# Decode attention on one core: the first K tile loaded as two halves of the partitions, by two queues

## The chip, the cores and the metric

The kernel runs on one core of one Trainium2 chip. A core has five instruction streams: TensorE (PE, matrix products, its weight loads shown as PEld), VectorE (DVE), ScalarE (ACT), GpSimd (POOL) and SyncE (SP), which here only issues loads. They run on their own and meet at semaphores. Loads are issued by SyncE and by ScalarE, each of which has a queue of its own; 16 DMA engines move the data from the chip's memory (HBM) into the core's working memory, which has 128 partitions. The metric is the device time in microseconds (us): the median over runs, and less is better. Before the change it was 318.32 us, the median of 3 runs from 318.13 to 318.70.

## The reference

One step of decoding: 16 heads, one query row for each, 8192 keys and values of 256 numbers, all in bfloat16.

```python
B, H, Sq, Sk, D = 1, 16, 1, 8192, 256

def reference(q, k, v):
    scale = q.shape[-1] ** -0.5
    scores = jnp.einsum("bhqd,bhkd->bhqk", q, k) * scale
    p = _softmax(scores, axis=-1)
    return jnp.einsum("bhqk,bhkd->bhqd", p, v)
```

Each head's K and each head's V are 8192 x 256 x 2 bytes = 4096 KB. Every byte of them is used once.

## The kernel before, in words

**Tiles.** The 8192 keys of a head are laid over the 128 partitions, 64 consecutive keys in each (`J = 64`), so a partition's part of a head's K is one run of 64 blocks of 256 numbers, 32 KB. K has two buffers (`kbuf`, the halves for even and odd heads) and V has two (`vbuf`). One load fills a buffer; its rows are the partitions.

**The order of the loads.** SyncE issues all K and V loads in the order written out in `ORDER` (L16): k0, k1, v0, k2, v1, k3, v2 and so on to v15. `CUTS` (L15) says which tiles are cut into pieces along the 64 blocks, each piece a load of its own: k0 and k15 after block 34, and v13, v14 and v15. The first piece counts on the tile's own semaphore ("k0" is that of even heads, "k1" of odd ones), the second piece of a K tile on "kb". Before the load of head h from 2 on, SyncE waits until the buffer is free: for K until DVE has finished head h - 2 ("kd", L122) and POOL too ("tp", L123), for V until TensorE has used the V that stood there ("pr", L125). SyncE's loads share one queue and are served in the order of issue. q is loaded by ScalarE (L387), 16 rows of 512 bytes, in ScalarE's queue.

**Scores.** TensorE spreads a head's q over the 128 partitions into `qrow` (L247), and ScalarE copies it into `q_now` (`q_copy`, L351 to L356, counting "qb"). Blocks 0 to 23 of K are multiplied with `q_now` by POOL, four blocks in one instruction (L186), into `prod`, and summed by ScalarE (L398). Blocks 24 to 63 are multiplied and summed by DVE with `qrow`, one block in one instruction, in four chunks of ten (L207 to L221). POOL and DVE both begin a head with `k_waits` (L141 to L144): q copied, and the head's K tile landed. DVE's chunks also wait for "kb" (L209), which for chunk 0 of head 0 is satisfied and from chunk 1 on stands for the second piece of k0, and for head 15 likewise for that of k15. The counter "kb" starts at 16 (L22).

**The rest.** DVE takes the largest score of each partition (L229), TensorE and DVE the largest of all (L332, L203), ScalarE the exponentials (L363), and TensorE multiplies them with V (`doubles`, L270) two heads behind the scores. ScalarE and TensorE collect the head's result. The last head's V is used in pieces as they land (L334 to L347), and SyncE stores the results at the end.

**At the start.** ScalarE issues the load of q, loads its table for the exponential, copies q for head 0 (`q_copy(0)`), and enters its loop, whose first act is `q_copy(1)`. In the code `q_copy` is called with a plain number only for head 0; in the loop its argument is the loop's register.

Of the kernel before, what the change touches and what calls it, by code (L numbers as in the profile page):

```python
# [11 lines left out]
NPL = 24  # L12
GRP = 4
CH = 10
CUTS = {"k0": (0, 34), "k15": (0, 34), "v13": (0, 48), "v14": (0, 40), "v15": (0, 28, 48, 60)}  # L15
ORDER = "k0 k1 v0 k2 v1 k3 v2 k4 v3 k5 v4 k6 k7 v5 k8 v6 k9 v7 k10 v8 k11 v9 k12 v10 k13 v11 k14 v12 k15 v13 v14 v15"  # L16
LAST_PAIRED = 28
STRIP = 64
# [7 lines left out]
def bass_standalone__mha_softmax__decode_kernel(nc: bass.Bass, q: bass.AP, k: bass.AP, v: bass.AP, out: bass.AP):  # L26
    B, H, Sq, D = q.shape
    Sk = k.shape[2]
    P = 128
# [25 lines left out]
    with contextlib.ExitStack() as ctx:  # L55
# [9 lines left out]
        def sem(name):  # L65
            if name not in sems:
                sems[name] = ctx.enter_context(nc.semaphore(name))
            return sems[name]
# [37 lines left out]

        for name in ("pool", "cb", "cf", "ldq", "qp", "qb", "tp", "sp", "kd", "m", "mT", "g", "bc", "nb", "ex"):
            sem(name)
        for name in ("rc", "pr", "cm", "pv", "fin", "o"):
            sem(name)  # L110
        for _, _, _, _, name in stream:
            sem(name)
# [1 line left out]
        def src(t, h):  # L114
            return t[0, h].rearrange("(p j) d -> p (j d)", p=P)

        @(lambda f: f(nc.sync))
        def _(sp):
            for kind, h, a, b, name in stream:
                if h >= 2 and a == 0:  # L120
                    if kind == "k":
                        sp.wait_ge(sem("kd"), (h - 1) * NC)  # L122
                        sp.wait_ge(sem("tp"), (h - 1) * NG)  # L123
                    else:
                        sp.wait_ge(sem("pr"), h + 2)  # L125
                buf = kbuf[:, h % 2 * J * D :] if kind == "k" else vbuf[h % 2]
                sp.dma_start(buf[:, a * D : b * D], src(k if kind == "k" else v, h)[:, a * D : b * D]).then_inc(  # L127
                    sem(name), 16
                )
            sp.wait_ge(sem(stream[-1][-1]), 16)  # L130
            sp.wait_ge(sem("fin"), LAST + 3)
            sp.dma_start(
                out.rearrange("b h s (two d) -> two (b h s) d", two=2)[:, 0:LAST, :],
                o_all[0:WIDE:BLK, :].rearrange("two (h d) -> two h d", d=HW),
            ).then_inc(sem("o"), 16)
            sp.wait_ge(sem("fin"), H + 4)
            sp.dma_start(out[0, LAST, :, :], o_last[:, :]).then_inc(sem("o"), 16)
            sp.wait_ge(sem("o"), 32)
            sp.nop()
# [55 lines left out]
        @(lambda f: f(nc.vector))  # L195
        def _(dve):
            def recips(h, n, after=0):
                dve.wait_ge(sem("pr"), h - n + (3 + after))
                dve.reciprocal(recip[:, ds(back(h, n), 1)], tot[0:WIDE, :]).then_inc(sem("rc"), 1)  # L199

            def xmax(h, n):
                dve.wait_ge(sem("mT"), h - n + 2)
                dve.tensor_reduce(g[:, :], mx[0:1, 0:P], AX.X, ALU.max).then_inc(sem("g"), 1)  # L203

            with dve.Fori(0, H) as h:
                par = dve.snap(h % 2)
                with dve.Fori(0, NC) as c:  # L207
                    k_waits(dve, h)
                    dve.wait_ge(sem("kb"), (h * 8 + c + 119) // 120 * 16 + 16)  # L209
                    for b in range(CH):  # L210
                        col = kbuf[:, ds(par * (J * D) + c * (CH * D) + (NPL + b) * D, D)]
                        ins = dve.scalar_tensor_tensor(  # L212
                            out=col,
                            in0=col,
                            scalar=SCALE,
                            in1=qrow[:, ds(par * 512, D)],
                            op0=ALU.mult,
                            op1=ALU.mult,
                            accum_out=S[:, ds(h * J + c * CH + (NPL + b), 1)],
                        )  # L220
                    ins.then_inc(sem("kd"), 1)  # L221
                    with dve.If(c == 0):
                        with dve.If(h > 1):
                            recips(h, 2)
                        with dve.If(h > 0):
                            xmax(h, 1)
                dve.wait_ge(sem("kd"), h * NC + NC)
                dve.wait_ge(sem("sp"), h * NG + (NG + 2))
                dve.tensor_reduce(m[:, :], S[:, ds(h * J, J)], AX.X, ALU.max).then_inc(sem("m"), 1)  # L229
            recips(LAST, 1)  # L230
            xmax(LAST, 0)
            recips(LAST, 0, 1)
            dve.wait_ge(sem("pv"), H + 4)
            dve.wait_ge(sem("rc"), H + 3)
            row, a = halves[1]
            dve.tensor_scalar(
                out=o_last[:, a : a + HW],
                in0=ob[row : row + 1, 0:HW],
                scalar1=recip[0:1, LAST:H],
                scalar2=None,  # L240
                op0=ALU.mult,
            ).then_inc(sem("fin"), 1)
# [106 lines left out]
        @(lambda f: f(nc.scalar))  # L349
        def _(act):  # L350
            def q_copy(h):  # L351
                act.wait_ge(sem("qp"), h + 1)
                par = 0 if isinstance(h, int) else act.snap(h % 2)
                act.activation(out=q_now[:, ds(par * D, D)], in_=qrow[:, ds(par * 512, D)], func=ACT.Copy).then_inc(  # L354
                    sem("qb"), 1
                )  # L356

            def expo(h, n):
                act.wait_ge(sem("bc"), h - n + 2)
                act.activation(out=negb[:, :], in_=sm, func=ACT.Copy, scale=-1.0).then_inc(sem("nb"), 1)  # L360
                act.wait_ge(sem("nb"), h - n + 2)
                i = back(h, n)
                act.activation(  # L363
                    out=E[:, ds(i % 2 * EW, J)].rearrange("p (two x) -> p x two", two=2),
                    in_=S[:, ds(i * J, J)].rearrange("p (x two) -> p x two", two=2),
                    func=ACT.Exp,
                    bias=negb[:, :],
                    scale=1.0,
                    accum_out=lsum[:, :],
                ).then_inc(sem("ex"), 1)  # L370

            def collect(h, n):
                act.wait_ge(sem("pr"), h - n + 4)
                act.activation(out=comb[:, :], in_=acc[0:ROWS, :], func=ACT.Copy).then_inc(sem("cm"), 1)  # L374

            def final(h, n):
                act.wait_ge(sem("pv"), h - n + 4)
                act.wait_ge(sem("rc"), h - n + 4)
                i = back(h, n)
                act.activation(  # L380
                    out=o_all[:, ds(i * HW, HW)],
                    in_=ob[0:WIDE, 0:HW],
                    func=ACT.Copy,
                    scale=recip[:, ds(i, 1)],
                ).then_inc(sem("fin"), 1)

            act.dma_start(q_sb[:, :], q[0, :, 0, :]).then_inc(sem("ldq"), 16)  # L387
            act.preload_act_table(ACT.Exp)
            q_copy(0)
            with act.Fori(0, H + 2) as h:  # L390
                with act.If(h < H):
                    q_copy(h + 1)
                with act.Fori(0, NG) as i:
                    with act.If(h < H):
                        act.wait_ge(sem("tp"), h * NG + i + 1)
                        for b in range(GRP):
                            part = prod[:, ds(i % 2 * (GRP * D) + b * D, D)]
                            ins = act.activation(  # L398
                                out=part,
                                in_=part,  # L400
                                func=ACT.Copy,
                                scale=SCALE,
                                accum_out=S[:, ds(back(h, 0) * J + i * GRP + b, 1)],
                            )
                        ins.then_inc(sem("sp"), 1)
                    with act.If(i == 1):
                        with act.If(h > 0):
                            with act.If(h < H + 1):
                                expo(h, 1)
                        with act.If(h > 2):  # L410
                            final(h, 3)
                with act.If(h > 1):
                    collect(h, 2)
            act.wait_ge(sem("pv"), H + 4)
            act.wait_ge(sem("rc"), H + 3)
            act.activation(out=o_last[:, 0:HW], in_=ob[0:1, 0:HW], func=ACT.Copy, scale=recip[0:1, LAST:H]).then_inc(
                sem("fin"), 1
            )
            act.nop()
# [28 lines left out]
```

## Time and profile before

| | |
|---|---|
| median of 3 runs | 318.32 us (318.13 to 318.70) |
| the profiled execution | 318.05 us |
| its span, first to last instruction | 316.6 us |
| busy: DVE, POOL, ACT, PE | 232.5, 204.3, 191.2, 147.2 us |
| data moved | 134.25 MB, mean 424 GB/s over the span |
| share of the DMA engines' time, SyncE's queue | 98.9% |
| loads of 4096 KB, issue to landing (median) | K 21.1 us, V 27.1 us |

The span is cut into 40 equal slices of 7.9 us for the busy digits; a digit is the busy share of a slice in tenths. The DMA digit is the mean over the core's 16 DMA engines. In the groups of instructions a row gives the line, the engine and the operation, what is written and what is read, the count, the busy time with the mean of one, and the idle time before them with what ended most of it. In the timeline a row begins with the start and the duration in us; several instructions of one kind in a row are merged ("x3"). "SPq" and "ACTq" are the sequencers of SyncE and ScalarE issuing loads. In the table by stretches a row gives the stretch, its length, the busy time of PE, PEld, DVE, ACT and POOL with their counts of instructions, then the clock that TensorE was granted, the share of the DMA engines' time that is busy, and GB/s.

### The profile page before, as it was taken

What the parts mean: (1) busy time and instruction counts of PE and PEld (TensorE: products, weight loads), DVE (VectorE), ACT (ScalarE), POOL (GpSimd) and SP (SyncE); (2) the same over time, 40 slices, a digit from 0 to 9 for tenths busy, and PEclk for the clock granted to TensorE, in tenths of its full rate; (3) what the DMA queues carried; (4) which work ended last, traced back from release to release, by engine and by line L of the source; (5) the groups of instructions that cost most, each with busy time, mean ns of one, the idle gap of its engine ahead of it and who ended that gap; (6) DMA issues with size and microseconds to landing.
All of it is one profiled execution on the core that took longest, in us unless ns stands there. A gap on an engine that the chain in (4) does not pass through costs nothing.

```text
span 316.6 us, 7885 instructions
## 1 busy us (share of the span) xinstructions
PE 147.2 (46%) x866; PEld 67.0 (21%) x866; DVE 232.5 (73%) x1329; ACT 191.2 (60%) x866; POOL 204.3 (65%) x115
## 2 busy tenths in 40 slices
PE   3201418264262633729191541915428063281977
PEld 1000103022120311314040210402213031130434
DVE  0797979497694967969797969769396793969700
ACT  2476737477373864767767657647386473858521
POOL 3888658395683857869686848568284783886400
PEclk9999999759585585766768585765958558576799
DMA  7999999999999999999999999999999999999996
GB/s 304 430 460 402 460 418 443 426 435 443 418 443 418 455 406 460 402 464 397 464 397 464 397 464 397 464 402 460 402 460 406 455 426 435 408 437 419 433 424 268
DMA packets 5683, 134.25 MB, mean 424 GB/s; under 512 B 673, under 2 KB 690, under 8 KB 946
## 3 DMA queue, kind: packets, MB, share of 16 engines
q1 hardware_dynamic: 5650, 134.23, 98.9%
q8 instruction: 1, 0.02, 0.0%
q10 hardware_dynamic: 32, 0.01, 0.0%
HBM read 134.23 MB, written 0.01 MB: 424 GB/s over the span
## 4 chain that ended last, share of the span: by engine, by line
DMA 52%; DVE 20%; issue 11%; DVEq 9%; PE 2%; POOL 2%; ACT 1%; SPq 1%; ACTq 1%; POOLq 1%
DMA kbuf<-in_k_dram 38%; DVE kbuf L212 19%; DMA vbuf<-in_v_dram 14%; DVEq L212 6%; PE acc L270 2%; POOL prod L186 2%; DVEq L209 1%; ACT prod L398 1%; DVEq L207 1%; DVEq L144 1%; SPq L127 1%; DVEq L143 0%; PE ob L339 0%; ACTq L398 0%; DVE g L203 0%
## 5 line engine op out<-in xcount | busy, mean ns | idle before, releaser
L212 DVE SCALAR_TENSOR_TENSOR kbuf<-kbuf,qrow x640 | 223.7, 416 | 53.7 <-issue 27.7
L186 POOL TENSOR_TENSOR prod<-kbuf,q_now 128x1024 f32 x96 | 201.8, 2123 | 89.7 <-DMA kbuf<-in_k_dram 60.7
L398 ACT ACTIVATE prod<-prod x384 | 154.5, 403 | 74.0 <-POOL prod L186 68.0
L270 PE MATMUL acc<-vbuf,E 128*64 128x512 bf16 x494 | 87.2, 529 | 30.3 <-DMA vbuf<-in_v_dram 29.7
L398 ACT ACTIVATION_READ_ACCUMULATOR prod<-prod x384 | 71.6, 186 | 0.0
L270 PEld LDWEIGHTS acc<-vbuf,E 128*64 128x64 bf16 x494 | 37.1, 150 | 74.1 <-issue 36.0
L212 DVE DVE_READ_ACCUMULATOR kbuf<-kbuf,qrow x640 | 52.6, 82 | 0.0
L317 PE MATMUL mx<-g,ones_row 1*128 1x1 f32 x34 | 9.7, 351 | 75.7 <-DVE g L203 75.4
L294 PE MATMUL ob<-comb,sel 97*1 97x128 f32 (+1 forms) x144 | 20.9, 321 | 35.0 <-ACT comb L374 34.8
L317 PEld LDWEIGHTS mx<-g,ones_row 1*128 1x128 f32 x34 | 8.2, 298 | 79.9 <-DVE g L203 79.2
L354 ACT ACTIVATE q_now<-qrow (+1 forms) x17 | 6.5, 383 | 28.8 <-PE qrow L247 28.7
L281 PE MATMUL spare<-ident 128*128 128x512 f32 x36 | 22.2, 700 | 0.0
L294 PEld LDWEIGHTS ob<-comb,sel 97*1 97x1 f32 (+1 forms) x144 | 8.0, 95 | 57.0 <-ACT comb L374 48.0
L332 PE MATMUL mx<-ident,m 128*1 128x128 f32 x32 | 7.8, 333 | 20.9 <-DVE m L229 20.9
L229 DVE TENSOR_REDUCE m<-S 128x1 f32 x16 | 3.5, 220 | 13.8 <-ACT prod L398 12.6
L374 ACT ACTIVATE comb<-acc 97x512 f32<-97x512 f32 x16 | 9.3, 578 | 6.2 <-PE tot L257 6.2
L363 ACT ACTIVATE E<-S,negb x16 | 9.3, 582 | 4.1 <-ACT negb L360 4.1
L199 DVE RECIPROCAL recip<-tot 33x1 f32 (+1 forms) x16 | 2.5, 155 | 9.8 <-PE tot L257 9.8
L247 PE MATMUL qrow<-q_sb,identb 16*128 16x256 bf16 x18 | 5.9, 337 | 4.6 <-DMA q_sb<-in_q_dram 4.6
L332 PEld LDWEIGHTS mx<-ident,m 128*1 128x1 f32 x32 | 2.9, 95 | 21.9 <-DVE m L229 21.9
L380 ACT ACTIVATE o_all<-ob,recip 33x128 f32 x15 | 5.4, 362 | 1.5 <-PE ob L294 1.5
L281 PEld LDWEIGHTS spare<-ident 128*128 128x128 f32 x36 | 5.8, 201 | 0.3
(27 smaller groups left out, 31.1 us busy)
## 6 DMA issues: line engine op xcount, KB each, us to landing
kbuf<-in_k_dram SPq DMA_DIRECT2D x14, 4096.0 KB, 21.1
vbuf<-in_v_dram SPq DMA_DIRECT2D x13, 4096.0 KB, 27.1
kbuf<-in_k_dram SPq DMA_DIRECT2D x2, 2176.0 KB, 13.3
kbuf<-in_k_dram SPq DMA_DIRECT2D x2, 1920.0 KB, 17.4
vbuf<-in_v_dram SPq DMA_DIRECT2D x1, 3072.0 KB, 29.9
vbuf<-in_v_dram SPq DMA_DIRECT2D x1, 2560.0 KB, 19.4
vbuf<-in_v_dram SPq DMA_DIRECT2D x1, 1792.0 KB, 10.3
vbuf<-in_v_dram SPq DMA_DIRECT2D x1, 1536.0 KB, 22.7
```

The lines of the kernel that those rows point to most:

```text
L186: pool.tensor_tensor(out=prod[:, b * GRP * D : (b + 1) * GRP * D].rearrange("p (b d) -> p b d", b=GRP), in0=kbuf[:, ds(par * (J * D) + i * ...
L212: ins = dve.scalar_tensor_tensor(out=col, in0=col, scalar=SCALE, in1=qrow[:, ds(par * 512, D)], op0=ALU.mult, op1=ALU.mult, accum_out=S[:, ...
L247: pe.matmul(qrow[:, ds(at * 512, D)], lhsT=identb[0:H, col].to_broadcast([H, P]), rhs=q_sb[:, :], start=True, stop=True,).then_inc(sem("qp ...
L270: ins = pe.matmul(acc[at : at + STRIP, :], lhsT=E[:, par * EW + j // 2 :][:, 0:STRIP], rhs=vbuf[par][:, j * D : (j + 2) * D], start=(j < 4 ...
L281: pe.matmul(spare[:, :].rearrange("p (b x) -> p b x", x=P), lhsT=ident[:, :], rhs=ident[:, :].rearrange("p (b x) -> p b x", b=1).to_broadc ...
L294: ins = pe.matmul(ob[row : row + wide, 0:HW], lhsT=sel[:, n * WIDE : n * WIDE + wide], rhs=comb[:, n * D + a : n * D + a + HW], start=(n = ...
L317: pe.matmul(sm, lhsT=ones_row[:, :], rhs=g[:, :], start=True, stop=True).then_inc(sem("bc"), 1)
L332: pe.matmul(mx[0:1, 0:P], lhsT=m[:, :], rhs=ident[:, :], start=True, stop=True).then_inc(sem("mT"), 1)
L354: act.activation(out=q_now[:, ds(par * D, D)], in_=qrow[:, ds(par * 512, D)], func=ACT.Copy).then_inc(sem("qb"), 1)
L363: act.activation(out=E[:, ds(i % 2 * EW, J)].rearrange("p (two x) -> p x two", two=2), in_=S[:, ds(i * J, J)].rearrange("p (x two) -> p x ...
L374: act.activation(out=comb[:, :], in_=acc[0:ROWS, :], func=ACT.Copy).then_inc(sem("cm"), 1)
L398: ins = act.activation(out=part, in_=part, func=ACT.Copy, scale=SCALE, accum_out=S[:, ds(back(h, 0) * J + i * GRP + b, 1)],)
```

## The change

K0 is no longer cut along its blocks. It is loaded in one piece of 64 blocks, but by two queues: SyncE loads partitions 0 to 63, ScalarE loads partitions 64 to 127, right behind its load of q. SyncE's half counts on "k0" as before, ScalarE's on a new semaphore, "half". `q_copy(0)` waits for "half"; POOL and DVE wait for that copy ("qb") and for "k0", and so for both halves. The wait for "kb" in DVE's loop is written anew, since only k15 has a second piece now: it is at 16, which it holds from the start, until chunk 1 of head 15, and 32 from there. All other loads, their order and their waits are as they were.

```diff
-CUTS = {"k0": (0, 34), "k15": (0, 34), "v13": (0, 48), "v14": (0, 40), "v15": (0, 28, 48, 60)}
+TWO_QUEUES = ("k0",)
+CUTS = {"k15": (0, 34), "v13": (0, 48), "v14": (0, 40), "v15": (0, 28, 48, 60)}
...
-        for name in ("rc", "pr", "cm", "pv", "fin", "o"):
+        for name in ("half", "rc", "pr", "cm", "pv", "fin", "o"):
             sem(name)
...
                 buf = kbuf[:, h % 2 * J * D :] if kind == "k" else vbuf[h % 2]
-                sp.dma_start(buf[:, a * D : b * D], src(k if kind == "k" else v, h)[:, a * D : b * D]).then_inc(
-                    sem(name), 16
-                )
+                rows = P // 2 if f"{kind}{h}" in TWO_QUEUES else P
+                sp.dma_start(
+                    buf[0:rows, a * D : b * D], src(k if kind == "k" else v, h)[0:rows, a * D : b * D]
+                ).then_inc(sem(name), 16)
...
-                    dve.wait_ge(sem("kb"), (h * 8 + c + 119) // 120 * 16 + 16)
+                    dve.wait_ge(sem("kb"), (h * NC + c + 3) // J * 16 + 16)
...
             def q_copy(h):
+                if isinstance(h, int):
+                    act.wait_ge(sem("half"), 16)
                 act.wait_ge(sem("qp"), h + 1)
...
             act.dma_start(q_sb[:, :], q[0, :, 0, :]).then_inc(sem("ldq"), 16)
+            act.dma_start(kbuf[P // 2 :, 0 : J * D], src(k, 0)[P // 2 :, :]).then_inc(sem("half"), 16)
             act.preload_act_table(ACT.Exp)
             q_copy(0)
```

## The prediction

> **What bounds the kernel now.** I read the DMA view first, because K and V are read once, 134 MB in all, and little is computed per byte.
>
> ```profile
> PE 147.2 (46%) x866; PEld 67.0 (21%) x866; DVE 232.5 (73%) x1329; ACT 191.2 (60%) x866; POOL 204.3 (65%) x115
> ...
> DMA  7999999999999999999999999999999999999996
> GB/s 304 430 460 402 460 418 443 426 435 443 418 443 418 455 406 460 402 464 397 464 397 464 397 464 397 464 402 460 402 460 406 455 426 435 408 437 419 433 424 268
> ...
> q1 hardware_dynamic: 5650, 134.23, 98.9%
> q10 hardware_dynamic: 32, 0.01, 0.0%
> ```
>
> The 16 DMA engines are busy in every slice but the first and the last. q1 is SyncE's queue and carries everything; q10 is ScalarE's and carries only q. The compute engines stand at 73% or less. The same in stretches (the columns that matter are the last two, DMA share and GB/s):
>
> ```profile
> 0.00:1.00 1.00, 0.00 (x0) 0.00 (x0) 0.00 (x0) 0.00 (x0) 0.21 (x4) 1.00 0.00 0
> 1.00:2.00 1.00, 0.00 (x0) 0.00 (x0) 0.00 (x0) 0.83 (x1) 0.02 (x1) 1.00 0.72 157
> 2.00:3.00 1.00, 0.00 (x0) 0.00 (x0) 0.00 (x0) 0.46 (x1) 0.63 (x3) 1.00 0.73 176
> 3.00:4.00 1.00, 0.00 (x0) 0.00 (x0) 0.00 (x0) 0.00 (x0) 0.99 (x7) 1.00 0.88 372
> 4.00:9.00 5.00, 4.12 (x14) 1.66 (x15) 0.00 (x0) 0.77 (x2) 0.72 (x7) 1.00 0.99 423
> 60.00:120.00 60.00, 28.31 (x156) 12.45 (x152) 43.47 (x249) 35.66 (x163) 37.85 (x18) 0.67 0.99 428
> 180.00:240.00 60.00, 27.57 (x161) 12.65 (x159) 47.15 (x272) 36.50 (x169) 40.29 (x20) 0.67 1.00 430
> 240.00:290.00 50.00, 21.99 (x131) 10.14 (x127) 37.30 (x216) 31.57 (x145) 33.91 (x17) 0.70 1.01 432
> 313.90:316.60 2.70, 1.06 (x32) 0.87 (x32) 0.34 (x1) 0.36 (x1) 0.00 (x0) 1.00 0.02 7
> ```
>
> From 4 us on the share is 0.99 to 1.01 at about 432 GB/s: 134.23 MB / 432 GB/s = 310.7 us, which with the start and the 2.7 us after the last load fills the span of 316.6. One load of 4096 KB (4.19 MB) costs 4.19 / 0.432 = 9.7 us of this stream. So whatever lengthens or interrupts the stream is paid in full at the end, and whatever compute does costs nothing until a load is issued too late. The chain of waits does name DVE:
>
> ```profile
> DMA 52%; DVE 20%; issue 11%; DVEq 9%; PE 2%; POOL 2%; ACT 1%; SPq 1%; ACTq 1%; POOLq 1%
> ```
>
> That is because the issue of a K load waits until DVE has left the buffer. But such a load then stands behind others in its queue, so DVE is on the chain without setting the time.
>
> ```profile
> L212 DVE SCALAR_TENSOR_TENSOR kbuf<-kbuf,qrow x640 | 223.7, 416 | 53.7 <-issue 27.7
> ```
>
> DVE sat idle for 53.7 us before its products, so it catches up when it is late.
>
> **The change part by part.** K0 now, and what its landing starts:
>
> ```profile
> 0.73 0.41 ACTq L387 DMA_DIRECT2D q_sb<-in_q_dram  x1
> 0.74 1.35 SPq L127 DMA_DIRECT2D kbuf<-in_k_dram  x3
> 1.20 11.78 DMA kbuf<-in_k_dram
> 9.13 4.20 POOL L186 TENSOR_TENSOR prod<-kbuf,q_now 128x1024 f32 x2 [4.13 <-DMA kbuf<-in_k_dram]
> 9.42 0.42 DVE L212 SCALAR_TENSOR_TENSOR kbuf<-kbuf,qrow  x1 [9.42 <-issue]
> 13.60 0.42 DVE L212 SCALAR_TENSOR_TENSOR kbuf<-kbuf,qrow  x1 [0.68 <-DMA kbuf<-in_k_dram]
> 5.01 0.90 ACT L354 ACTIVATE q_now<-qrow 128x256 bf16<-128x256 f32 x2 [2.55 <-PE qrow L247]
> 24.33 0.33 SPq L127 DMA_DIRECT2D kbuf<-in_k_dram  x1
> 24.33 17.79 DMA kbuf<-in_k_dram
> 40.88 0.33 SPq L127 DMA_DIRECT2D kbuf<-in_k_dram  x1
> 53.33 0.33 SPq L127 DMA_DIRECT2D vbuf<-in_v_dram  x1
> 57.73 0.33 SPq L127 DMA_DIRECT2D kbuf<-in_k_dram  x1
> ```
>
> *The early start is removed.* Blocks 0 to 33 let POOL and DVE begin at 9.1 and 9.4; all of K0 is there at 1.20 + 11.78 = 12.98, and DVE's second chunk restarts at 13.60. With one piece both begin after K0's last byte, and after the wait below. DVE's work on head 0 runs from 9.42 to the issue of K2 at 24.33 less a stall of 0.68, so 14.2 us; POOL's is 18.27 + 4.21 - 9.13 = 13.4, inside it:
>
> ```profile
> 18.27 4.21 POOL L186 TENSOR_TENSOR prod<-kbuf,q_now 128x1024 f32 x2 [0.36 <-issue]
> ```
>
> *The new wait.* q_copy(0), which ended before 5.9, now waits for ScalarE's half. Queued behind it on ScalarE are q_copy(1) and the sums of head 0, which need POOL anyway. POOL and DVE wait for q_copy(0) by "qb", and they need that half too, so the wait adds only the copy (0.9 us for two, 0.45 for one) and a hop: they begin at about 13.6 + 0.6 = 14.2 if K0 lands when it does now. TensorE's first pass waits for none of these.
>
> *Where the 4.8 us go.* Head 0 then ends at 14.2 + 14.2 = 28.4, and that is when K2 can be issued, 4.1 us later than 24.33. K2 lands at 24.33 + 17.79 = 42.12, and its own transfer is 9.7, so its first byte is due at 32.4. The first DMA follows its issue by 1.20 - 0.74 = 0.46: 28.9 against 32.4 leaves 3.5 us. K3 goes from 40.88 to some 45 and is due one V load after K2 (42.12 + 9.7 = 51.8); V2 from 53.33 to at most 57.4, due at 61.5; K4 from 57.73 to at most 61.8, due at 71. By head 3 the loss is gone, out of DVE's 53.7 us of idle time. The early start costs 0; without that queue of issued loads it would cost 4.1.
>
> *Issue.* SyncE issues one load fewer (1.35 / 3 = 0.45 us each), ScalarE one more behind q, at 0.73 + 0.41 = 1.14. Its table load of 1.28 us slips by 0.45, unseen before 5.01. Cost 0. The ramp: from 1.2 to 4.0 some 157 + 176 + 372 KB per us moved, 0.705 MB, worth 1.6 us at full rate, so 1.2 us are lost there. [...] The longer rows themselves: 423 GB/s with K0's cut rows against 432, at most 2% of 9.7 us, 0.2; I take 0.
>
> *The two halves.* This is the unknown. All loads now span 128 partitions, so the 16 engines write to all 128 at once: 432 / 16 = 27 GB/s by each engine, 432 / 128 = 3.4 GB/s into each partition. The change makes each transfer span 64. Is a narrow transfer still spread over all engines? q spans 16 partitions, and q10 shows 32 packets for it: 16 rows and 16 completions, so one of each per engine. Hence every engine gets 4 rows of SyncE's half and 4 of ScalarE's, and a moment in which all engines are at rows of one half asks 6.8 GB/s of each partition written. If the ceiling of 432 belongs to the engines, K0 still takes 9.7 us: 0. If it belongs to what lies in front of the partitions, a half flows at 216 GB/s, and as both queues are served in turn by the same 16 engines in step, K0 takes up to 19.4: +9.7. No row shows a transfer of 64 partitions, so both ends stay. [...] The engines don't start in one instant, though, and SyncE's rows start 0.4 us ahead of ScalarE's, so that at times some write to one half while others write to the other. I take 8.5 of the 9.7, a judgement.
>
> [...]
>
> *Sum:* 0 (early start) + 0 (issue, ramp, rows) + 8.5 (halves). The profiled execution took 318.05 (its span of 316.6 and 1.45 around it), close to the median of 318.32. 318.05 + 8.5 = 326.5. DVE and POOL would then start near 14.2 + 8.5 = 22.7, K2 be issued at 36.9 and be due at 40.9: still in time.
>
> **The rivals.**
>
> *No change, 318.0 (317.7 to 318.6).* The ceiling is the engines' own; K0 takes 9.7 us through two queues as through one. For it: rows of 17 KB and of 32 KB move at nearly one rate, as an engine's own limit would have it. [...] This is the case on the other side of my forecast: it decides if 64 partitions can take 432 GB/s, or if the two queues fall out of step, so that eight engines write to one half while eight write to the other. [...]
>
> *Faster, 317.2 (316.8 to 317.6).* The ramp is cut: about 0.8 of the 1.2 us lost before 4 us. For it: 157 and 176 GB/s in the first two us. Against: the share there is 0.72, so the engines are mostly waiting on their first packets, not without work.
>
> *In part, 319 to 323.5.* The halves conflict, but the engines are half out of step: 1 to 5.5 of the 9.7.
>
> *A hole in the queue, 319 to 330.* ScalarE's half is served only after what SyncE has queued, or late enough that K2 comes after 32.4. With SyncE's half of K0, K1 and V0 ahead of it, 10.5 MB, it would land near 30 and K2 be issued near 45, some 12 us late. Against: q went by that queue while SyncE's loads ran, and landed long before K0 did:
>
> ```profile
> q_sb<-in_q_dram ACTq DMA_DIRECT2D x1, 8.0 KB, 3.8
> ```
>
> **How the numbers follow.** The forecast, 326.5 (own range 324 to 328.3, as 6 to 10 us of K0): 0.52. No change: 0.25. Faster: 0.09. In part: 0.10. A hole: 0.04. Something below or above 0.2% (0.64 us) is about what a measurement of this kernel can tell from no change. Faster 0.09, same 0.25, slower 0.52 + 0.10 + 0.04 = 0.66. For 8 in 10 the range goes from 317.5, within the faster case, to 328.3, the forecast with the whole 9.7 and half a us for the extra hops.
>
> **What would show it.** In the changed profile: POOL's first product at some 22.7 rather than 9.13 (14.2 if the halves don't conflict); between 2 and 20 us a rate of 216 to 250 GB/s with a DMA share still near 1, and 432 from then on; the issue of K2 near 37, with no slice of low share after it; q10 with 2.1 MB. The forecast is wrong if K0 lands at 13 as before; the step on K2 is wrong if the DMA share drops between 28 and 45 us; the step on the early start is wrong if the end moves by more than K0's own delay.

## The result and the profile after

The changed kernel takes 331.81 us (median of 4 runs, 331.33 to 333.07) against 318.35 us: a ratio of 1.043, 95% interval 1.040 to 1.046. It is slower by 13.5 us, where 8.2 were forecast against the median. The profiled execution took 331.48 us with a span of 329.5. The time lies above the forecast range, which ended at 328.3.

The page of the changed kernel: DMA busy digits and rates, the two queues, and the loads of K0's halves (line, operation, count, size, us from issue to landing).

```profile
DMA  9899989999999999999999999999999999999996
GB/s 192 191 255 446 446 318 446 442 386 446 446 426 402 446 446 446 426 402 434 446 434 414 438 442 438 430 414 442 434 442 422 422 446 434 417 420 424 433 423 253
...
q1 hardware_dynamic: 5442, 132.13, 95.4%
q10 hardware_dynamic: 112, 2.11, 2.9%
...
kbuf<-in_k_dram SPq DMA_DIRECT2D x1, 2048.0 KB, 17.6
...
kbuf<-in_k_dram ACTq DMA_DIRECT2D x1, 2048.0 KB, 24.6
```

For the first two slices, 16 us, the DMA engines are busy and yet move 191 GB/s: busy does not mean fast. In the sixth slice they are idle for a part, at 318 GB/s. From there on the page is that of before. The same in stretches (us from the start; the last two columns are the DMA share and GB/s):

```profile
1.00:2.00 1.00, 0.00 (x0) 0.00 (x0) 0.00 (x0) 0.25 (x1) 0.01 (x1) 1.00 0.03 8
4.00:9.00 5.00, 3.52 (x12) 1.53 (x13) 0.00 (x0) 0.00 (x0) 0.72 (x7) 1.00 1.02 210
13.00:18.00 5.00, 0.00 (x0) 0.00 (x0) 0.00 (x0) 0.00 (x0) 0.00 (x0) 1.00 0.99 210
23.00:28.00 5.00, 0.00 (x0) 0.00 (x0) 0.63 (x3) 0.77 (x2) 0.95 (x1) 1.00 1.01 406
38.00:43.00 5.00, 0.22 (x2) 0.09 (x2) 4.13 (x25) 3.41 (x16) 4.64 (x4) 1.00 0.73 315
43.00:48.00 5.00, 0.68 (x3) 0.10 (x1) 3.70 (x21) 3.68 (x17) 3.25 (x2) 1.00 1.11 419
```

Three things differ from before: 210 GB/s instead of 423 while K0 comes in, no row of K0 before 2 us (8 GB/s between 1 and 2 is q; before, 157 GB/s of K0 moved there; the first row starts at 2.1 us instead of 1.8), and a hole between 38 and 43 us. The timeline has what belongs to the hole:

```profile
25.77 0.38 ACT L358 ACTIVATE q_now<-qrow 128x256 bf16<-128x256 f32 x1 [22.73 <-DMA kbuf<-in_k_dram]
27.05 4.20 POOL L188 TENSOR_TENSOR prod<-kbuf,q_now 128x1024 f32 x2 [22.04 <-ACT q_now L358]
27.37 0.42 DVE L214 SCALAR_TENSOR_TENSOR kbuf<-kbuf,qrow  x1 [27.37 <-ACT q_now L358]
42.03 0.33 SPq L129 DMA_DIRECT2D kbuf<-in_k_dram  x1
71.53 0.33 SPq L129 DMA_DIRECT2D vbuf<-in_v_dram  x1
```

ScalarE's half lands at 25.7, the copy of q follows, DVE begins at 27.37 and frees the buffer for K2 at 42.03, when the loads ahead of K2 have just run out: between 41.25 and 43.0 us no row starts, and K2's first rows move 1.0 us after its issue.

### The profile page after: what moved, and what is told of

It reads as the page before. It is cut to its first block, busy times and chain, and to the rows that moved or that the text cites. A ratio compares the mean times of both kernels' runs of the same rounds, so it can differ in the third digit from the quotient of the medians.

```text
span 329.5 us, 7886 instructions
## 1 busy us (share of the span) xinstructions
PE 147.2 (45%) x866; PEld 67.0 (20%) x866; DVE 232.5 (71%) x1329; ACT 191.0 (58%) x866; POOL 204.3 (62%) x115
## 4 chain that ended last, share of the span: by engine, by line
DMA 51%; DVE 20%; issue 12%; DVEq 10%; PE 2%; POOL 2%; ACT 1%; ACTq 1%; POOLq 0%; SPq 0%
DMA kbuf<-in_k_dram 37%; DVE kbuf L214 20%; DMA vbuf<-in_v_dram 14%; DVEq L214 6%; PE acc L272 2%; POOL prod L188 2%; DVEq L211 1%; ACT prod L403 1%; DVEq L209 1%; DVEq L146 1%; DVEq L145 0%; SPq L129 0%; PE ob L341 0%; ACTq L403 0%; DVE g L205 0%
## 5 line engine op out<-in xcount | busy, mean ns | idle before, releaser
L364 ACT ACTIVATE negb<-mx 128x1 f32<-128x1 f32 x16 | 2.5, 158 | 6.0 <-PE mx L319 6.0
```

## The experiments

The edits are shown against the changed kernel, with "..." where lines are left out; the four kernels that load K0 in pieces of the partitions on SyncE's queue alone were built from the kernel before, with the same rewritten wait for "kb". Each run's median is compared with runs of the kernel before on the same chip (318.28 to 318.37 us; 318.82 in one single run).

| kernel | us | above before |
|---|---|---|
| the change | 331.81 | 13.5 |
| K0 uncut, one queue | 320.07 (318.12 to 320.94) | 1.8 |
| K0 by blocks, two queues | 324.68 | 6.4 |
| halves, one queue | 331.21 | 12.9 |
| partitions 32 to 95, 0 to 31, 96 to 127 | 325.34 | 7.1 |
| four quarters (one run) | 329.83 | 11.0 |
| even, then odd partitions (one run) | 319.32 | 0.5 |
| K0, K1 and V0 by blocks, two queues | 323.37 | 5.0 |
| the change, products half as wide | 329.62 | 11.3 |
| by blocks, products half as wide | 321.03 | 2.7 |
| uncut, products half as wide | 318.20 (318.01 to 318.63) | -0.1 |
| the change with even and odd partitions | 321.30 (320.63 to 323.35) | 2.9 |

### The cut alone is taken away

```diff
-TWO_QUEUES = ("k0",)
+TWO_QUEUES = ()
...
-                if isinstance(h, int):
-                    act.wait_ge(sem("half"), 16)
...
-            act.dma_start(kbuf[P // 2 :, 0 : J * D], src(k, 0)[P // 2 :, :]).then_inc(sem("half"), 16)
```

> K0 in one uncut piece over all 128 partitions, on SyncE's queue alone, with no wait on ScalarE: the cut is gone, the halves are not there. If the early start of head 0 is worth nothing (the prediction's step): K0 takes 9.7 us of the stream, POOL starts near 13.5 instead of 9.1, K2 is issued near 28, the DMA share stays near 1 from 28 to 45 us, 318.3 us (317.6 to 318.9). If the early start does carry some of the loss (rival): a low DMA share between 28 and 45 us and 319 to 322 us.

Ten runs from 318.12 to 320.94, median 320.07; ratio 1.0038 (1.0016 to 1.0059). By the medians it is 1.8 us above the kernel before, by the means 1.3. Three equal the kernel before (318.1 to 318.3), one is at 319.1, and six are at 320.0 to 320.9. Timeline and stretches of the profiled execution, which took 320.82:

```profile
13.73 4.20 POOL L188 TENSOR_TENSOR prod<-kbuf,q_now 128x1024 f32 x2 [8.71 <-DMA kbuf<-in_k_dram]
28.68 0.33 SPq L129 DMA_DIRECT2D kbuf<-in_k_dram  x1
58.24 0.33 SPq L129 DMA_DIRECT2D vbuf<-in_v_dram  x1
```

```profile
28.00:33.00 5.00, 0.91 (x3) 0.18 (x3) 2.93 (x18) 3.22 (x16) 3.62 (x2) 1.00 1.08 465
61.00:64.00 3.00, 1.15 (x11) 0.50 (x11) 1.22 (x8) 1.43 (x6) 1.83 (x1) 1.00 0.80 306
```

K2 is in time, as predicted (28.68, no dip). But V2 goes out at 58.24 instead of 53.33, 4.9 us later, and the stream dips to 306 GB/s between 61 and 64. A stretch of 3 us is coarse (one row on each engine is 0.52 MB, 175 GB/s of it), but the single packets say the same: from 60.9 to 62.6 us one to three of the 16 engines have nothing to move, though V2 went out more than 2 us before its first rows were wanted. Such a dip costs more than its mean share shows, because the end waits for the last engine: in the kernel before, all engines stop within half a us near 313.4; here the share falls to 0.60 from 314.3 us on and 0.32 from 315.0 on, as they finish one after the other. So the early start is not free: it keeps a margin that some executions without it lack. Neither of the two expectations held alone.

### Two queues without halves

```diff
-                rows = P // 2 if f"{kind}{h}" in TWO_QUEUES else P
+                if f"{kind}{h}" in TWO_QUEUES:
+                    b = J // 2
...
-            act.dma_start(kbuf[P // 2 :, 0 : J * D], src(k, 0)[P // 2 :, :]).then_inc(sem("half"), 16)
+            act.dma_start(kbuf[:, J // 2 * D : J * D], src(k, 0)[:, J // 2 * D :]).then_inc(sem("half"), 16)
```

> K0 by two queues as in the change, with the same wait on ScalarE, but split along its 64 blocks: SyncE loads blocks 0 to 31 and ScalarE 32 to 63, each over all 128 partitions. If the loss comes from transfers that span only half of the partitions: about 430 GB/s from 4 us on, K0 landed near 14, and 318 to 319 us. If it comes from two queues taking turns on the same DMA engines, whatever the partitions: about 215 GB/s until 22 us as in the change, and 329 to 332 us.

324.68 us, 1.019 (1.016 to 1.022): between the two. The rate is full, and yet 6.4 us are lost. Stretches and loads of this kernel:

```profile
4.00:9.00 5.00, 4.12 (x14) 1.66 (x15) 0.00 (x0) 0.00 (x0) 0.73 (x7) 1.00 1.00 429
28.00:33.00 5.00, 0.00 (x0) 0.00 (x0) 4.91 (x31) 3.70 (x17) 4.39 (x3) 1.00 0.64 275
33.00:38.00 5.00, 0.91 (x3) 0.19 (x3) 2.98 (x18) 3.22 (x16) 4.00 (x2) 1.00 0.61 210
```

```profile
kbuf<-in_k_dram SPq DMA_DIRECT2D x1, 2048.0 KB, 9.8
kbuf<-in_k_dram ACTq DMA_DIRECT2D x1, 2048.0 KB, 16.6
```

SyncE's part is there after 9.8 us, ScalarE's after 16.6: once SyncE's part is through, its queue goes on with K1, and the two queues share the DMA engines in turns, as the single packets of the change show (rows of ScalarE's queue start from 9.4 us, of SyncE's from 11.8, of ScalarE's from 14.1). ScalarE's part also begins later: its first row starts at 5.4 us, SyncE's at 1.8. All data flow at full rate, but K0 is complete at 17.8 instead of 13, K2 is issued at 34.10 against a turn near 31, and the stream stands with a share of 0.6 from 28 to 38 us; against 430 GB/s this is worth some 4.4 of the 6.4 us.

### Halves without a second queue

```diff
-            act.dma_start(kbuf[P // 2 :, 0 : J * D], src(k, 0)[P // 2 :, :]).then_inc(sem("half"), 16)
...
+                if f"{kind}{h}" == "k0":
+                    for n, (lo, hi) in enumerate(PIECES):
+                        sp.dma_start(buf[lo:hi, 0 : J * D], src(k, 0)[lo:hi, :]).then_inc(
```

with `PIECES = ((0, 64), (64, 128))`, on a semaphore each; `q_copy(0)` waits for all pieces but the first.

> K0 in the same two halves of the partitions, both on SyncE's queue, one after the other; ScalarE's copy of q waits for the second. If half of the partitions can take only half of the rate: some 215 GB/s for 19.4 us, K0 landed near 21.5, so some 4 us before the 25.7 of the changed kernel, because no K1 rows stand between; DVE starts near 23 and K2 is issued near 37.5, in time for its turn at 41, so no hole; 327.5 to 328.7 us. If the two queues are the cause: 318.3 us.

331.21 us, 1.040 (1.037 to 1.043), as slow as the change within the spread, so a second queue is not needed for the loss. Its stretches:

```profile
4.00:9.00 5.00, 3.52 (x12) 1.53 (x13) 0.00 (x0) 0.00 (x0) 0.72 (x7) 1.00 1.02 210
38.00:43.00 5.00, 0.91 (x3) 0.18 (x3) 2.97 (x18) 2.97 (x14) 4.64 (x3) 1.00 1.01 419
72.00:75.00 3.00, 0.95 (x11) 0.49 (x11) 2.13 (x13) 2.00 (x9) 1.50 (x1) 1.00 0.85 295
```

The rate is the 210 GB/s of the change. There is no hole before K2, as expected, but one at 72 to 75, where V2 is due (issued at 69.98). It ended 2.5 us above the expected range: the hole at 72 to 75 is worth some 0.9 us of that (295 GB/s against 430), and K0 landed at 24.4 and not at 21.5; how the rest divides was not followed up.

### Which partitions: the middle half, quarters, even and odd

The same kernel with `PIECES = ((32, 96), (0, 32), (96, 128))`:

> K0 in three pieces on SyncE's queue: partitions 32 to 95, then 0 to 31, then 96 to 127. [...] If each partition has its own limit of 3.4 GB/s: 9.7 us for each of the three, 29 us together, 338 us. If the width plays no role: 318.3 us.

325.34 us, 1.022 (1.021 to 1.024): neither 338 nor 318.3. The rates differ from piece to piece:

```profile
3.00:7.00 4.00, 1.96 (x7) 1.18 (x6) 0.00 (x0) 0.00 (x0) 1.71 (x12) 1.00 0.92 393
8.00:16.00 8.00, 1.78 (x9) 0.53 (x8) 0.00 (x0) 0.00 (x0) 0.00 (x0) 1.00 0.99 209
```

Partitions 32 to 95, also 64 of them, come in at the full rate (393 GB/s between 3 and 7 us, the ramp and the last rows in it), 0 to 31 and 96 to 127 at 209; by the single packets, a row of 32 KB takes 1.2 us in the first piece and some 2.5 in the other two. At 209 GB/s the two outer pieces, 2.1 MB, take 10.0 us instead of 4.9 at 430, which is 5.1 of the 7.1 us lost; the rest was not followed up. With `((0, 32), (32, 64), (64, 96), (96, 128))`:

> K0 in four quarters of 32 partitions on SyncE's queue, one after the other. [...] If the rate falls with the number of partitions: 108 GB/s, K0 after 39 us, 348 us or more.

One run, 329.83 us against 318.82; the stretch of its K0:

```profile
4.00:23.00 19.00, 4.72 (x16) 1.84 (x16) 0.00 (x0) 0.00 (x0) 0.73 (x7) 1.00 0.99 214
```

32 partitions on one side of 64 are as fast as 64 of them (214 GB/s here, 210 with the halves). And with the even partitions first, then the odd ones (`buf[lo:P:2, ...]`, `lo` 0 and 1). The "paths" in this expectation and the next stand for whatever holds a load on one side of partition 64 to 210 GB/s; what that is, no run shows:

> K0 in two pieces on SyncE's queue: the even partitions, then the odd ones, 64 rows each. Each piece reaches every path. If reaching all paths is enough: 430 GB/s, K0 landed near 14, 318.2 to 321 us. [...]

One run, 319.32 us against 318.82, as expected:

```profile
4.00:13.00 9.00, 4.29 (x14) 1.71 (x14) 0.00 (x0) 0.00 (x0) 0.72 (x7) 1.00 1.06 459
```

Full rate with 64 partitions (a row counts in the stretch in which it starts, so that a short stretch can show more than 432). So neither the count of partitions nor that of rows decides, but whether the rows lie on both sides of partition 64: 393 GB/s for 32 to 95 and 459 for every other partition, against 209 to 214 for halves and quarters. What sets this limit is not shown: a partition always holds the same 32 KB of K0, so every run that chose partitions also chose which part of HBM is read, and these runs don't tell a limit in front of the partitions from one at the memory.

### The change with its geometry alone undone

```diff
-                rows = P // 2 if f"{kind}{h}" in TWO_QUEUES else P
+                step = 2 if f"{kind}{h}" in TWO_QUEUES else 1
...
+                    buf[0:P:step, a * D : b * D], src(k if kind == "k" else v, h)[0:P:step, a * D : b * D]
...
-            act.dma_start(kbuf[P // 2 :, 0 : J * D], src(k, 0)[P // 2 :, :]).then_inc(sem("half"), 16)
+            act.dma_start(kbuf[1:P:2, 0 : J * D], src(k, 0)[1:P:2, :]).then_inc(sem("half"), 16)
```

> The changed kernel in all but one thing: SyncE loads the even partitions of K0 and ScalarE the odd ones, in place of the lower and the upper half. Rows, queues and the wait are the same. If the halves' own price is that each reaches only half of the paths: some 430 GB/s from 4 us on; ScalarE's last row is the ninth of its DMA engine, so K0 has landed near 15, DVE starts near 17, K2 is issued near 31 against a turn near 32, with a hole of up to 1.5 us: 319.3 to 322 us. If two queues that take turns are slow whatever the partitions: near 215 GB/s and 330 to 332 us.

321.30 us, 1.009 (1.006 to 1.012), within the expected range. Same queues, rows and wait, and 10.5 us of the 13.5 are gone. Of the 2.9 us that stay, some 1.5 are the dip around K2, which goes out at 31.91 (354 GB/s between 28 and 33 and 380 in the five us behind, against 430); the rest was not traced:

```profile
4.00:9.00 5.00, 3.52 (x12) 1.53 (x13) 0.00 (x0) 0.00 (x0) 0.72 (x7) 1.00 1.08 465
28.00:33.00 5.00, 0.35 (x2) 0.09 (x2) 4.01 (x23) 3.41 (x16) 4.64 (x4) 0.50 0.87 354
```

A second queue won nothing in these runs (K0 uncut 320.07 us in one queue, by blocks 324.68 in two), and it can cost: the part in the second queue lands late when the first queue has more to do (14.4 us after its issue here, and 10.1 for SyncE's part; 16.6 and 9.8 by blocks).

### Lateness: three tiles in step, and narrower products

K1 and V0 are split by blocks over both queues too, so that neither queue runs ahead (their consumers wait for both parts):

```diff
-TWO_QUEUES = ("k0",)
+TWO_QUEUES = ("k0", "k1", "v0")
...
+            act.dma_start(kbuf[:, (J + J // 2) * D : 2 * J * D], src(k, 1)[:, J // 2 * D :]).then_inc(sem("half1"), 16)
+            act.dma_start(vbuf[0][:, J // 2 * D : J * D], src(v, 0)[:, J // 2 * D :]).then_inc(sem("halfv"), 16)
```

> As the split of K0 by blocks over both queues, but K1 and V0 are split over both queues in the same way, so that SyncE's queue never runs ahead of ScalarE's. If the split by blocks lost its 6.4 us because ScalarE's part of K0 had to share turns with K1, which stood behind SyncE's part: K0 has landed near 14, DVE starts near 15, K2 is issued near 29.5, and the time is that of the uncut piece, 318.2 to 321 us. If a second queue costs by itself: 324 us or more.

323.37 us, 1.015 (1.014 to 1.017): only 1.4 us of the 6.4 came back, so this expectation missed. K0 landed at 15.5 rather than 17.8, but not at 14, and the wait on ScalarE costs more than I had put down:

```profile
15.50 0.38 ACT L361 ACTIVATE q_now<-qrow 128x256 bf16<-128x256 f32 x1 [11.38 <-DMA kbuf<-in_k_dram]
17.29 0.42 DVE L216 SCALAR_TENSOR_TENSOR kbuf<-kbuf,qrow  x1 [17.29 <-ACT q_now L361]
```

From landing to DVE's first product 1.8 us, so K2 went out at 32.48, still late (a share of 0.74 between 28 and 33). The queues were not in step either: ScalarE's first row starts at 5.5 us, SyncE's at 1.8, so that SyncE's queue reaches K1 while ScalarE's part of K0 still has rows left. Sharing turns with K1 is thus still a part of the lateness, the copy behind the wait another.

To see lateness by itself, compute was made lighter in three kernels: DVE, POOL and ScalarE use 128 of the 256 columns, for instance

```diff
-                        col = kbuf[:, ds(par * (J * D) + c * (CH * D) + (NPL + b) * D, D)]
+                        col = kbuf[:, ds(par * (J * D) + c * (CH * D) + (NPL + b) * D, HW)]
```

> K0 uncut on SyncE's queue, with the products on 128 of 256 columns (half of each dot product left out). If the 318.1 to 320.9 us of the uncut piece are holes of some 2 us before V2 and later loads in some executions: no hole, no spread, 318.0 to 318.6 us, the time of the kernel before, since the stream of loads alone sets it. If the uncut piece is slower in itself: near 320 us.

318.20 us, ten runs from 318.01 to 318.63, ratio 0.9996 (0.9987 to 1.0006): the loss and the spread of the uncut piece are both gone, with V2 issued at 53.50 instead of 58.24. So its 1.8 us come from loads that compute lets go too late.

> The changed kernel with all loads and waits as they are, but DVE, POOL and ScalarE use only the first 128 of the 256 columns of each product (half of each dot product is left out, its sums are those of the first half). If part of the loss is a late issue of K2 and of later loads, because head 0 begins late and takes 14 us: K2 is issued near 37 to 39 instead of 42.0, before its turn at 41.8, the DMA share stays near 1 from 38 to 43 us, and the time is that of the halves alone, 328.5 to 329.8 us. If lateness of compute plays no role: 331.3 to 332.2 us.

329.62 us, 1.036 (1.034 to 1.038): the time came as expected, 2.2 us less than the change. K2 moved less than expected, to 40.76, since DVE still took 13.3 us for head 0: it stood for 1.4 to 1.7 us before each of its last three chunks, 4.6 us in all, without a wait that the profile names. That is enough:

```profile
40.76 0.33 SPq L129 DMA_DIRECT2D kbuf<-in_k_dram  x1
```

```profile
38.00:43.00 5.00, 0.91 (x3) 0.18 (x3) 2.57 (x22) 0.38 (x1) 0.86 (x1) 1.00 1.08 419
```

where the change has a share of 0.73 and 315 GB/s.

> The split of K0 by blocks over two queues, with the products on 128 of 256 columns (half of each dot product left out). If its 6.4 us were all holes before loads that are issued late: K2 is issued near 30 instead of 34.1, against a turn at 31, and 318.2 to 320.5 us. If a second queue costs by itself: near 324 us.

321.03 us, 1.009 (1.007 to 1.011), half a us above the range: head 0 got only 1.3 us shorter, K2 went out at 32.83 rather than 30, and a part of the hole stayed (a share of 0.71 between 28 and 33). Most of the 6.4 us is lateness; that all of it is was not shown.

## Why the prediction was wrong

**What bounds the kernel: right.** The stream of loads sets the time; with lighter compute the uncut piece has the time of before to 0.1 us.

**The two halves: the half rate was right, the term too small.** I put K0 at 8.5 us more, between 0 and 9.7, as some engines would be out of step. They weren't: all 16 engines take rows of one queue and then of the other (the rows that start between 2.2 and 9.3 us are SyncE's alone, the 16 from 9.3 to 10.3 all ScalarE's), and the rate was 210 GB/s, not more than the 216 of a strict half. So K0 took some 4.19 / 0.210 = 20.0 us, +10.3. Undoing the geometry alone gave 10.5. That two queues would mix the halves was the reason for the discount, and one queue with two halves is as slow as two. The row that would have excluded it did not exist before; the upper bound should have been taken. The 8.5 itself was a judgement that no run shows; the runs gave 10.3 and 10.5. That the limit lies in front of the partitions, the case that the term stood on, is not shown either (above).

**"The early start costs 0" and "K2 in time": wrong, and the larger failure of reasoning.** K2 went out at 42.03, 5.1 us after the 36.9 foreseen, and the loads ahead of it ran out: the drop of the DMA share between 28 and 45 us that the prediction named as its sign of being wrong is there, 0.73 from 38 to 43. Most of the 5.1 is the landing of ScalarE's half, foreseen at 12.98 + 8.5 = 21.5 and seen at 25.7. Its first row starts only at 9.4 us, behind three of SyncE's rows on every engine, and before it is complete SyncE's queue goes on with K1: two rounds of K1's rows, at 19.0 and 22.9 us, come in between. The rivals had only the whole queue ahead of it. From landing to DVE's first product 14.2 - 12.98 = 1.2 us were foreseen and 1.6 measured, and DVE's head 0 took 14.7 us instead of 14.2. The margin was also too large on paper. I took the turn from the landing of K2, 32.4, while its first rows start at 31.6 in the kernel before; and I took 0.46 us from issue to first DMA, where K2's first rows came 1.0 us after the issue. That is some 1.4 us. V2 was put at 57.4 with a turn at 61.5 in the case without a conflict; with the uncut piece it went out at 58.24, and that was too late for some of the engines. Price: 13.5 - 11.3 = 2.2 us in the change, by the kernel with narrower products, of which the hole from 38 to 43 is some 1.3; and 1.8 in the uncut piece.

**"Issue 0, ramp 0": nearly.** The 0 for the ramp was a judgement that no run shows; in its place K0's first row starts at 2.1 us, 0.3 us later than before.

**The sum by the runs:** 10.3 (halves) + 2.2 (late loads) + 0.3 (first rows) = 12.8 of the 13.5 measured; 0.7 is left open.

**The rivals.** "No change" fell: 64 partitions on one side took 210 GB/s, not 432, and the two queues didn't fall out of step. "In part" fell, "faster" fell. "A hole in the queue" happened beside the forecast rather than in its place: the two were not alternatives, and the range should have held their sum.

## What to carry to other kernels

Where the stream of loads is the bound, split a load along its columns or take every other partition, never the lower and the upper half of the partitions: 0 to 63 or 64 to 127 alone got half the rate here (210 GB/s, against 429 by blocks and 459 by every other partition), and neither a second queue nor a second piece made up for it. A load that is issued "in time" needs a margin against the first row that is wanted, not against its landing, and more than the 2 us or so that V2 had in the uncut piece; a late start of compute spends that margin, first on one buffer's load and then on the next. A part of a tile in a second queue lands late when the first queue goes on with other work (16.6 us after its issue by blocks, where the first queue's part took 9.8), so the tile is complete only then.

## What the runs showed that I had not expected

A first load of 64 rows starts late: in all six kernels that begin so (the change, the halves, the middle half, even and odd in two forms, the lighter change), its first row starts at 2.1 to 2.2 us; with 128 rows, and with 32, at 1.8. Issuing such a load took 0.6 us, and so did the load right behind it (1.22 for the half and K1 in the change, 0.87 for K0 and K1 uncut). The runs don't show why.

Small lateness costs by chance. The uncut piece, with one and the same order of loads, took from 318.12 to 320.94 us in ten runs, the kernel before from 318.06 to 318.82 in the thirteen beside it: where a load goes out just about when it is wanted, some executions lose some 2 us and others nothing. The kernel before had one such run too: of ten on another chip, nine took 318.29 to 318.83 us and one 320.93; it was not profiled, so what it lost is not known.
